# Four x buffers instead of three, earlier load slots, and a new table of turns in a fused Fourier layer and MLP

## The chip, the cores and the metric

The kernel runs on one core of a Trainium2 chip. The core has five engines that work from their own instruction queues, each in order: TensorE (PE in the profile, with its weight loads as PEld), VectorE (DVE), ScalarE (ACT), GpSimd (POOL) and SyncE (SP). SP and POOL issue the DMA transfers of this kernel, which run on 16 DMA engines. TensorE writes into PSUM banks of 512 fp32 columns, and ACT or DVE must empty a bank before TensorE can use it again. The metric is the device time of one execution in microseconds; lower is better. A table of runs gives the median of several executions; the profile is one further execution.

## What is computed

Two stages run one after the other. The first works on 8 sequences of 3008 positions and 256 channels: a Fourier transform along the sequence, one complex 256 x 256 product, a soft threshold, and the inverse transform. The second treats the 24,064 resulting rows as tokens of an MLP with 2048 hidden units whose activation is a squared relu.

```python
X = np.fft.rfft(x, axis=1)                   # x: (8, 3008, 256)
Yr = Xr @ w_r - Xi @ w_i + b_r
Yi = Xr @ w_i + Xi @ w_r + b_i
Yr = np.sign(Yr) * np.maximum(np.abs(Yr) - 0.01, 0.0)   # Yi likewise
y = np.fft.irfft(Yr + 1j * Yi, n=3008, axis=1)
h = y.reshape(24064, 256) @ w_in             # w_in: (256, 2048)
r = np.maximum(h, 0.0)
out = (s * (r * r) + b) @ w_out              # w_out: (2048, 256)
```

## The kernel before

**The transform of one batch.** 3008 is 94 x 32, so the transform is a product of small Fourier matrices in four steps.

1. `s1_units(b)`: 16 units. Each multiplies a piece of x (94 partitions x 512 columns) by `A_t` into a PSUM bank and evicts it to a tile `u`. A tile of four positions is written to a DRAM buffer `ud` (L784).
2. `take_rows` reads `ud` back, turned, as four tiles `us` (L802), and `s23_units(b)` works on them: `fwd_unit` (matrix `F_t`, result `xf`), `sum_unit` and `mix_unit` (the complex product, with three real products in place of four, into `ring`), `shrink` (the soft threshold: three DVE instructions, L899, L903 and L907, then moves of quarters by SP, L918, or for the last pairs by DVE copies, L924), and `inv_unit` (matrix `T_t`, result `v`, written to the DRAM buffer `vd`, L955).
3. `take_half` reads `vd` back as two tiles `vs` in four transfers (L972).
4. `s4_units(b)`: 14 units with the matrix `C_t` write the rows `yt` that the MLP reads.

**The MLP.** Tokens are cut into tiles of 512. A tile has 16 slots, and in slot `mc` `first_mm` computes 128 hidden units of it: two matmuls of 512 columns into `psh`. After each second slot the two banks of `psh` get one relu (L1154 on ACT or L1156 on DVE, result `rt`) and one square (L1163 on ACT or L1165 on DVE, result `gt`). The second product of tile i runs in the slots of tile i+1. Most tiles use a scheme of seven block products in place of eight (`seven_mms`). It needs sums of quarters of `gt`, four for each half of a tile (`s_op`, L1325 on DVE); the fourth may also be an accumulating DMA from `gt` to `gt` issued by POOL (L1317). Results leave PSUM through L1390 or L1278 on DVE into `ost` and are stored by SP (L1189).

**The order around it.** The first batch is transformed alone (`first_batch`, about the first 46 us). From then on the units of the next batches' transforms are put into the slots of the MLP of earlier batches: `plan` and `aside` are dictionaries from a slot number to work, `mark[b]` is the first slot of batch b's own tiles, and in the loop over b the names `s0`, `s1`, `s2` are `mark[b-2]`, `mark[b-1]`, `mark[b]`. So step 1 of batch b runs from `s0 + 36` to some 14 slots ahead of `s1` (8 for b = 2), its rows are taken around `s1`, steps 2 and 3 run from `s1 + 2`, and step 4 in the last 15 slots ahead of `s2`. This fixes TensorE's order. Every instruction of another engine (an eviction, relu, square, sum, transfer) is a "piece": `later` appends it to `pieces`, and `TURNS` has one entry for each of the 2693 pieces, two base-36 digits whose value divided by four is a delay in pieces, and whose remainder is the engine (ACT, DVE, SP, POOL). `plan_turns` sorts the pieces by number plus delay, and `pump` emits them in that order between the matmuls.

**Buffers of x.** x of a batch is read from DRAM as four tiles, chunks of 8 positions, by POOL, with a conversion to fp16. From batch 2 on `load_x_later` issues each tile as two transfers, halves, of 188 KB in fp16 (L350). The tiles rotate through `xpool`, which has three buffers; the fourth chunk of batches 0 and 1 has a buffer of its own (`x2pool`), later used by `T_s`. With three buffers, the fourth chunk of a batch takes the place of its own first chunk, and its load waits for step 1 to have read that one. Only the first chunk of batch 2 has a gate: a one-element copy (L348) that waits for the `us` rows of batch 1.

Of the kernel before, what the change touches and what calls it, by code (L numbers as in the profile page):

```python
# [27 lines left out]
    "101c0x111515141h1l14181k3o181l1x5m5m750x151h1l2e2q1u1i0g0t0g0s7x0p0t11192y1q2226080w2g0h110l"
    "111h1p3e2m2u220h0t0g1c0x1h212d2i2q3a3q0h101g0g250h3q4q0l191l1x2m3m321q0c0w1g0c0p0x1d292x3q32"
    "3y36101w091e0c0p1h0o390x1h1p252m323q3a0k0s1831523i0l0x111l1t212e2u3m36080m0c0w0k1829182o1519"  # L30
    "1h1t362u3m260o0s1p101s111h1l1x263a2i2q15321k2g154e3q0o151d25292t45453l0c0k1k0l0t1h21292h292l"
    "2t081e0d0i0g3h0h0s212h143i1g1m1k1n371g1s2g1h3e4m101a2i2q3m3q0w120s0x1s113q101p0x111g1l1m181h"
    "1g1k201l3i4y1h1m252t1c3x1h191c451c1c20191e1x11143p1x191k2814151c1q192q141o2g1d1l1k2h1h4u1c1p"
    "1p1o1x2d2p1g1x4236181824152e1865141l11161e1x2h143415182p1b1c301t151i181p291d141p1h1k291p1o24"
    "1l1n6j1k2d1l1l1k1o1h2p1x261h1t1c1w1f5v1h1p1x2d2m2u2y3i101g0x160w1h2h0x2l0w181d0x1n1o2o1t110s"
    "1t1z1x1l1x292d2u2i3e2y0g1w1110182d182p1d1g1w1d1f5b1p1o202p1l1x1g1x1h2y1g1o1h292t454i564i5a18"
    "1u0o180l0u0h1l29101g0l143h0r111g2s1d0p0s1f1p0w142l111h184a191l21252d2u2m3u2u0w200w3q0w1h100t"
    "101t1c201p2p113t141i1p26191g1w1d1t1w281x261f4b1d1h252l1h25393h4q423i4214240l0k6y0r0s3u0s2k0t"
    "0l0o0z0l0t0w1l1011141o2k191h1p293p4l294l292t1x2p0g0u0k200l0w1i0l102d0x1t0x19264i1e102y1g2h0w"
    "1g1y1k28192q1i15292t181k2k1h151e3e3m1f2k2u142s1h0x1l1d141p18191g1t2m2a1o1y1o2g1d1p1s291p1p24"  # L40
    "1p2y1o1t1s1y1o211p1q252h1k1o2w1t1k1z1k1s3g1t1l1o1z1x1h1s291p1p1q1o1x241k1t242o1p3e1l1p1o1p2h"
    "1p2t1c1l2y1h1g2h1d1i1g1w1h1m252l1o2g1l2t391j1g311t1d1620291n1d141o1h1w1w1x20241p3f7b1l1t1l1x"
    "1o1s1d1p2h461h1p1c1s1b5v191l1t213q262e2u0w1g0t0y0w1h2h0x2t0w181d0x1n1s1w1p0x0w1t1n1p1p1t2l2p"
    "3a3m2m3q0w1g150w191g14291t181s191b5j1x1h1k1w1x211h1p252a1k1o1h252l495m4i4q4y0x1q0w180t0y111l"
    "2d101g0x0w190z15142g1h0x141j1h101l3c142h1k46191h1p252l3u2u3u2u0o0w111a0w28190x181918202d3l11"
    "191d3a253a191g1k1d1l1o201l1q174b19251x2d1d2t3d3l3u4m3y460o1g0x0o4i0z0k3u182w0p0h0k0v110p0o18"
    "0w1519181w191h292h3h2x4d4d4l49292h0l3a0o1w0d0o120l0o210p3x0k111a1y1e0t6m0s2c0w102a1c1x1d3a2a"
    "1a1m0x1x2p181c2s1l1c1m363u1j282m0s2k190p2t150w1l190x14282m4i191i1428111l1l211t2l1c1t2q1g2l1h"
    "1q1c1s191i2h2t1d1k3d1p1g1v1g202s1x1h181z1p1g1o2k1l1x1q1s1t211o1w202s1x1m1t1x1o1w2p1l1x1l1t2y"
    "1t1k281l1q1o211l1q252l1o381l2c351j1g2x1x191a1c1x1r1h18251l1s1w1w24281p1r7b1x251h1p1o2o1p1x1l"  # L50
    "3u1g1t1g2k1f5v1d1h1l1t22262y2i0s1d0t2y0o1p2h0w2t0w281d0p1j0w2k1p0x101t1n1p1p2d2h3l3u424a4m08"
    "1s0t0x0w1h101p1p141k11137719181c1w191d1c1l1p3m1o2k1d1l1p293q463a260w160w1g0x260t1t2h182g0p0t"
    "290z1514251x11181z251k1s2o1g211s3m1d1p1t252d3e3m42260w18112e1g2s100t1c151g1t113d193p1c1q1x36"
    "191c1p1h1k1k241l1u1b4r181l212d1l2l353p4e4u4i3q0s380t0s160z0k160s1c150t0s171d11101t101d1k1o24"
    "1l1p1x2t41413d3d2t4h393h0w160w1c0l0t0y0p142l11450l11524m3q1m1y0u005y042410101e101p151u1i120t"
    "1t2h1014281h181i3a3e2p2d2m0o2h190l3l150w140x11141k2m3u1t1y1c28191d1g211d3d1w1h2q1g1l1k1q1g1t"
    "1h22292t1c1g3c1x1g231g1k341x1d1k231p1g1k2k1l1p1q1p1t2h1o1t1s2s1p1q1s1x1o1s251p2h1l253y1k1k28"
    "1h2a1k1x1h1i212h1k3c1h242l1f1c2w1x15161g211r1p18241p1t2g1s1t2c1x1n7f1g1x1x1h1s2o1p1p1x4e1g1t"
    "1c2k1f5z1d1h1l1t2u1y2e3e0s1d0t1i0o1p2h0w2x0w341d0p1j0w1o1t0x101d1r1p1p1x2d2d2q362m3e0c1w0t10"
    "102g181d211g211d1f5b211o1o3h1p291k1t1h1q1c1s1l1p2t454i5e4q4y151a0s1g0t160s1p29101g0p103t0r11"  # L60
    "1g2o1d0p0s1f1h0w1g2c0w19192a1d1h252l2x4m3m322q111c103e18240x111415141s1t2h0x3h151q1t2e15141s"
    "1g1p202g1p1y1f4j1h1p252p1l292x3t4i4q423m142c0l0k0y0r0w3y0w240x0p0s0z190x0w280x191c1c2o1d1l1p"
    "25412x2d4d2p3t3t250o2u0o210l0x3u0l0o350p210k1d2q0s0y0o2p0w141m182c1d221g292p1c1o2w1l1o1y3a3a"
    "452d2m1429190p2h150w1s0x1114281u3y1t221828191h1o1x1l21201p2y1c241l1u1g1x1d1u2h2t1k1s3o1p1d1v"
    "1g1o2k1x1h1k1z1x1l1c2l1p1t1m1t1w241l1s212k1p421o1t1k1o2g2h351d1h1q1c1d211c261g1s1d1i212d1o34"
    "1p202l351c301p155y181t1j19101p1h1k211p1o241x1n771g251l1l1k1s1h1p214q1h1t1c1s1b5v1d1h21253q32"
    "2i260s140p0u0l212h0w1l0s180p0t2t1c2g1p0x1c1l1n1p1h252l393u3e3y46081g0x0w191g141t19182d19135b"
    "1d141c1w191t1c1x212y1g291h1p2h3x4q564a3q0s1u0s180p0u0s1h1x101k0x142x0v0x1g2k1h110s311d141828"
    "191l1l6e1l1p1x2h2t3a4e3m2q0w19103i101k180t0s11181s1d2h0x3x141e1h2y0x181o151l1s201h1q174b1925"
    "252h192x3d3p3y4u4e3y0o340d0w4a0n0o0y0o180t0l0o0z1d0t0s1p10191g1k1w1h1x2d2p49354h414h412p2d0d"  # L70
    "120o180l0s2a0p101o0x410h1p565a1u080u0h2c0o0s1q181x19222a362u121a0p1p2d0w102w1d141e363e252c2m"
    "0k28110h2x110o281w11151h2q2y1x261g28151l1c251h2d1l1x2y1k1o212a1k1x1h26252t181g301t1k1z1k1k2w"
    "1x1h1k2x1p1g1p2k1k1l1m1p1o2g1l1t1s2s1p3u1l1p1p1o2g1l1p1g253a1h1h211c2e1g1s1d1i21291o2g192l2p"
    "1j1k2o1l1d5m20291f151c201h1p251o1o201l1o2p1x1l1k1s1l3h1l3e1h1p1c1o1h1l1t2132363e2a0w1k0t0y0w"
    "1p21182p1c2k1t15231c3g211h181t391p1t1x252h323q322e0s0w1110151g10291t1g25151l201k1x2l311o1x1p"
    "3a1c1o1h2h454h525i5a4e111q0o180p0y0k1h1p141k0p141d0v19183119111f1h0w141c1o1x1519252935424a3i"
    "320o1o103y101g11151d1c1k0x1h112h1p2y19102c181c1x191y1c25252h1l2t393h4q4a3i3q0s2k111b0o4m0o10"
    "110p140z111d0w201d141c2c191h1p2h353d3l392h293l290g1o0l0p0u0l0o2c0t2h1d461i1u220o28151x261g1t"
    "1d2i221q212l20142g1518223a3e2d1c2h1l0t1n1d1g1w1h1g1p363a1k1s1l1p1s211h1l1l1u1k1t1w211t222h2t"
    "1k1o3c1p1h1v1g1o3d251h1k231h1g1k291l1p1p1o2g1o1s212o1l1k211p1o2o1p2l1k1p1u1l1p291k4d411k1w1h"  # L80
    "1m1x291k24191j1g2h1p191x1l1c1w1d1g251o281p1x1o1x21251x261g241o211p1y252h1o2c1l1r1o2o1x1h391t"
    "1k1o1p1p1t1s1w1p1t1w2d1l1t1x221k211s1w1x2225291s2t1d1r1s2g1t1l1v1l1o211t1w241s2g1p1t1s281p1p"
    "212a1l1x1o1w1x2225251s2c1d2h1o2g1p1h1v1l1s241t1t1x1w201t1x20291p1t1t2e2y1u1u321c1l1o1s1l1q21"
    "291o2g191n1s2o1t1l2t1p1o1o1p1p1t1s2c1p1t1s251p1t212u1o1t1s1w1p1u25291o2t1d1r1s2s1t1l1v1l1o1s"
    "1t1t241s2h1p1t1t1s1t1y1w281s251p1q1x1y21261p1u1x1y"
# [1501 lines left out]
```

## Time and profile before

| | us |
|---|---|
| median of 3 runs | 814.78 |
| lowest and highest | 814.72, 814.84 |
| profiled execution | 814.47 |
| its span, first to last instruction | 812.4 |
| mean granted TensorE clock in it | 0.997 of full |

The profile shows, for each engine, how long it was busy; for a group of instructions, the line, engine, operation, tiles (out<-in), count, then busy time and mean duration in ns, then the idle time before them and what ended it. A row of a timeline has the start, the duration and the instruction, with a count when several were merged; a bracket tells how long the engine sat idle before it and what released it. A row of the waits names who waited for whom, with the total, the number of times and the longest. SPq rows are the sequencer of SP issuing transfers.

The span has five main loads: 1792 of TensorE's matmuls write `psh` (444.5 us busy, with the later ones overlapping), 4,032 of them `psa` from `gt` (344.1 us in two groups); ACT has 347 relus (355.0 us) and 259 squares (272.2 us); DVE has 117 squares (141.2 us) and 279 sums (190.8 us in three groups). The 65 accumulating transfers take 4.0 us from issue to landing in the median, from 3.2 to 8.7. The halves of x issued on L350 take 5.5 us in the median, from 3.9 to 8.1.

### The profile page before, as it was taken

The page shows a single profiled execution, that of the slowest core. Times are in us where ns is not written, and L with a number is a line of the kernel's source. Part 1 is how long each engine was busy: PE and PEld are TensorE (multiplying, and loading weights), DVE is VectorE, ACT ScalarE, POOL GpSimd, SP SyncE. Part 2 cuts the span into 40 slices and gives each one's busy share as a digit, 9 for nine tenths or more (in the row PEclk, how much of TensorE's full clock was granted, in tenths as well). Part 3 has the DMA queues.
Part 4 walks back from the last instruction along what each step waited for, and adds up shares of the span by engine and source line. Part 5 has one row for each costly group of instructions (what it writes and reads, how often), then busy time and mean ns, then how long its engine had stood idle before and what let it go on. Part 6 is the DMA issues. An engine that isn't in the chain of part 4 may idle for free.

```text
span 812.4 us, 22159 instructions
## 1 busy us (share of the span) xinstructions
PE 801.9 (99%) x9006; PEld 614.0 (76%) x9006; DVE 760.4 (94%) x1334; ACT 748.9 (92%) x938; POOL 108.7 (13%) x153
## 2 busy tenths in 40 slices
...
GB/s 201 182 173 89 92 243 150 115 138 166 222 122 120 151 154 232 100 123 179 121 209 113 158 153 145 169 125 143 140 162 117 141 98 115 176 70 54 78 55 90
DMA packets 121054, 113.42 MB, mean 140 GB/s; under 512 B 9965, under 2 KB 98161, under 8 KB 120953
## 3 DMA queue, kind: packets, MB, share of 16 engines
...
## 4 chain that ended last, share of the span: by engine, by line
PE 55%; DVE 3%; DMA 1%; issue 0%; DVEq 0%
PE psh L225 24%; PE psa L225 20%; PE psf L225 11%; DMA gt<-gt 1%; DVE gt L1325 1%; DVE ost L1390 1%; DVE ring L924 1%; DVE gt L1165 0%; DMA out_dram<-ost 0%; DVE v L288 0%; DVE u L288 0%; DVE s L1325 0%; DVE rt L1156 0%; DVE ost L1278 0%; DVE ring L907 0%
## 5 line engine op out<-in xcount | busy, mean ns | idle before, releaser
L225 PE MATMUL psh<-yt,w_in 128*128 128x512 f16 (+3 forms) x1792 | 444.5, 343 | 0.2 <-ACT rt L1154 0.2
L225 PEld LDWEIGHTS <-gt 128*128 128x128 f16 x4400 | 306.5, 98 | 143.8 <-DVE gt L1325 3.9
L1154 ACT ACTIVATE rt<-psh 128x1024 f32<-128x1024 f32 x347 | 355.0, 1025 | 25.6 <-PE psh L225 22.9
L1163 ACT ACTIVATE gt<-rt 128x1024 f16<-128x1024 f32 x259 | 272.2, 1061 | 3.4 <-DVE rt L1156 1.4
L225 PE MATMUL psa<-w_out_t,gt 128*128 128x128 f16 (+1 forms) x2208 | 199.9, 224 | 0.3 <-DVE gt L1165 0.3
L225 PEld LDWEIGHTS <-w_in 128*128 128x128 f16 x1824 | 151.9, 98 | 15.9 <-issue 1.5
L225 PE MATMUL psa<-T_s,gt 128*128 128x128 f16 x1824 | 144.2, 219 | 0.3
L1165 DVE TENSOR_TENSOR gt<-rt 128x1024 f16<-128x1024 f32 x117 | 141.2, 1217 | 2.5 <-ACT rt L1154 2.1
L1317 POOL DMA_DIRECT2D gt<-gt x65 | 56.5, 868 | 574.2 <-DVE s L1325 157.7
L1390 DVE SCALAR_TENSOR_TENSOR ost<-psa,s_bc,bias_bc 128x256 f32<-128x256 f32 x152 | 72.8, 479 | 7.8 <-PE psa L225 6.7
L1325 DVE TENSOR_TENSOR gt<-gt 128x1024 f16<-128x1024 f16 x107 | 73.0, 683 | 0.6
L1390 DVE SCALAR_TENSOR_TENSOR ost<-psa,s_bc,ost 128x256 f32<-128x256 f32 x129 | 61.7, 478 | 4.8 <-PE psa L225 4.0
L880 DVE TENSOR_TENSOR ring<-psf,s 128x512 f16<-128x512 f32 x84 | 57.6, 686 | 4.0 <-PE psf L225 2.5
L1325 DVE TENSOR_TENSOR gt<-gt,s 128x1024 f16<-128x1024 f16 x86 | 59.0, 686 | 1.2 <-PE psf L225 0.4
L1325 DVE TENSOR_TENSOR s<-gt 128x1024 f16<-128x1024 f16 x86 | 58.8, 683 | 0.4 <-ACT gt L1163 0.2
L225 PEld LDWEIGHTS <-s 128*128 128x128 f16 x688 | 45.4, 98 | 17.6
L225 PE MATMUL psa<-T_s,s 128*128 128x128 f16 x688 | 52.4, 219 | 0.0
L225 PE MATMUL psf<-W_g,xf 128*128 128x256 f16 x336 | 50.4, 273 | 0.0
L225 PEld LDWEIGHTS <-xf 128*128 128x128 f16 x504 | 44.8, 98 | 3.3
L350 POOL DMA_DIRECT2D x<-in_x_dram x48 | 32.3, 766 | 78.6 <-PE psa L225 39.6
L225 PE MATMUL psf<-x,A_t 94*96 94x512 f16 x103 | 39.3, 381 | 0.3 <-DVE u L288 0.2
L225 PE MATMUL psf<-C_t,vs 96*128 96x96 f16 x484 | 38.3, 205 | 0.9 <-DMA vs<-vd 0.6
...
## 6 DMA issues: line engine op xcount, KB each, us to landing
...
ring<-ring SPq DMA_DIRECT2D x120, 64.0 KB
```

Source lines behind the costliest of these rows:

```text
L225: return nc.tensor.matmul(out, lhs, rhs, **how)
L350: nc.gpsimd.dma_start(out=t[0:N1, i * w : (i + 1) * w], in_=xv[:, at : at + w])
L880: lambda e: nc.vector.tensor_tensor(out=ring[0][:, i % 4], in0=ps, in1=hold[i // 2][:, i % 2].unsqueeze(1).to_broadcast([P, 2, D]), op=ALU ...
L924: lambda e, o=o[:, k], a=a[:, k]: nc.vector.tensor_copy(out=o, in_=a),
L1154: nc.scalar.activation(out=rt, in_=ps, func=AF.Relu)
L1163: nc.scalar.activation(out=gt, in_=rr, func=AF.Square)
L1165: nc.vector.tensor_tensor(out=gt, in0=rr, in1=rr, op=ALU.mult)
L1317: nc.gpsimd.dma_start(out=a12, in_=a11, accum_op=ALU.add)
L1325: nc.vector.tensor_tensor(out=out, in0=a, in1=b, op=op)
L1390: ins = nc.vector.scalar_tensor_tensor(out=out(), in0=hold[of], scalar=s_bc[0:size], in1=other(), op0=ALU.mult, op1=ALU.add,)
```

## The change

Three things change. `xpool` gets four buffers. The loads of x and of `us` rows get other slots: for batch 2 the fourth chunk is asked for at slot 24 and not 55; for batches 3 to 7 the four chunks at -8, -6, 10 and 26 slots from the mark of the batch two before, and not at 10, 14, 26 and a computed slot; the four row loads at -9, -6, -4 and -1, and not at -9, -6, -1 and 4. The table `TURNS` is new throughout: 2693 entries as before, the mean delay is 16.0 pieces and was 17.0, and 869 pieces go to ACT (875 before), 1269 to DVE (1261), 444 to SP (444) and 111 to POOL (113).

```diff
 TURNS = (
-    "1x1x261s291p1t221o291s1w291l1u2m2q2y321c1t1c1c25191c291d1s1c282w1o1t1k20353n6z3r6f173r111521"
...
+    "1t1t221o251l1p1y1k251o1s251h1q2i2q362q181p18181t151820181p1c203o1l201g1l294f7b1b3b1b3j15151h"
...
 )
@@
-    xpool = ctx.enter_context(tc.tile_pool(name="xp", bufs=3))
+    xpool = ctx.enter_context(tc.tile_pool(name="xp", bufs=4))
@@
-            assert b < 2 or (b, c) in held[-3:]
+            assert b < 2 or (b, c) in held[-4:]
@@
-    for c, at in enumerate((18, 18, 18, 55)):
+    for c, at in enumerate((18, 18, 18, 24)):
         aside.setdefault(at, []).append(
             lambda c=c: load_x_later(2, c, [] if c else [row_loads[(1, 3)]])
         )
@@
-        for q, at in enumerate((-9, -6, -1, 4)):
+        for q, at in enumerate((-9, -6, -4, -1)):
             aside.setdefault(s1 + at, []).append(lambda t=take_rows, q=q: t([q]))
@@
         if b + 1 < B:
-            free_at = 37 + 4 * (mark[b] - s1 - 50) // 16
-            for c, at in enumerate((10, 14, 26, free_at)):
+            for c, at in enumerate((-8, -6, 10, 26)):
                 aside.setdefault(s1 + at, []).append(
                     lambda b=b, c=c: load_x_later(b + 1, c)
                 )
```

The table's entries decide both where a piece stands in its engine's queue and which engine takes it, so nearly every queue is in a new order, while the matmuls stay in theirs.

More of the change, by code (lines that the diff above doesn't have):

```diff
@@ L26 @@
 TURNS = (
-    "1x1x261s291p1t221o291s1w291l1u2m2q2y321c1t1c1c25191c291d1s1c282w1o1t1k20353n6z3r6f173r111521"
[L28 to L85, printed above, removed]
+    "1t1t221o251l1p1y1k251o1s251h1q2i2q362q181p18181t151820181p1c203o1l201g1l294f7b1b3b1b3j15151h"
+    "101p1x0w11150w201h0w14182w192h3h5m564v7j590l0p0x111m12221i000h042c7h0d0l0p0t1u121a1y040o1o08"
@@ new lines @@
+    "0p0d0t19213e262e2q050p0w2c0l1519212a2y3a2e080s280c0l2t3y4a090p0t1h2a2y2i1m081029090l0t1h2529"
+    "3m4e2q2e0w1g002i040o191c3811191h1x3i2u1y420o0w181p4y260h0t0x1d1h1x262u361y04360s180p0x2p141s"
+    "11151d1h3e2q2a2u0g111l0w1g111h1t292e3e2e2q0t360s182p363e0l0x19191h413p2x31080w1t0c0p151t2d2d"
+    "352t35081e080q0c350k0w1k2k101y111a1c1k1l2k2d2i32141e2i2u3i4i0w160t0s1p153i101o0x1x141g1i151g"
+    "1l1k1s1h3m4y191i1t2p111s1t10181v15203s141m1x0x102l1p191p2t14181c1m1d2q101c341f63191l1c1s1h3e"
@@ new lines @@
+    "175n1d1d1h181l212l3u0x1h1q2y0s0s1w0p260s450s1d0t0y161l210w2w0x1w2h0z0w2k1h0t0w1h3t1d0w1w1d1l"
+    "1s1l1p201t1j5z1c1l1l1l1k1o1h1x1l321g1p1g2c1h1h1p212i36222i0s1s0p0u0s2d2l1g310p340x1517141s1x"
+    "19101h1v1t1x252935423m4a320g1p0x0w101c101p15141k150z5r1l15181w1d21181l192y1k2k1h1h1p2d3e2i3q"
+    "2q0s3q0o110p0y0k1l2d0w1k0t0w3t0z151s2d1p0x0w1v1l1c1s201g1x1l3q191l1t1x2h3m3a4m2e0s180w161828"
+    "0x11141518201529151p196q1t1y19181s1c1h1s241h1q1h21212h19212l3d463y4m3a10240d0c4a0n0o0y0o2d11"
@@ new lines @@
+    "0l0o13150p0s1k0w0x101k2k191h1p2149354d3125312d250c2y0g100h0p0y0p102g1t3d0h1p4i2a1u0c0u0g2k0w"
+    "1d2i1g25151e1m11212h0w1g2c1d1g1q3a3u3l2d2m0s2g190l1d11101l101114282e3y191i1420111h1l1x1l2p1g"
+    "1p1y1c1g1h1u1k24191u2d2h1d1o3k1d1h1j1k1o2k1t1h1g1r1h1p1g2k1h1l1m1p1x2h1j5v1c1l1k201h3y1f5z1c"
+    "1p1d1c1o1t251615192q1d141w151a181l15161t29182w191c291b182w1l1114211j1h101t1d1o291p1o241l1n6z"
+    "1k1t1l1t1k1t1l2h1t1y1c1l181o1h1x25293m2q2y260w1g0t0y0w1x29102h14240p0x39102g1p0x101h1n1p1h1p"
@@ new lines @@
+    "29313q363q3y0c1k0x0w1019181x15141g150z6z1l19181o1p1x151l213a1g1k1d1l1x1x2a363e3m0w3q0w180l1y"
+    "0s1l2d14380h0l150r11142s1l0x141r1h141h2s1c251d421h1h1p2d2h3y3i2u2e0o0x0w3m101s0x0l0w1h0w1k21"
+    "2d0l3t0x2m1l260t0w1k141h1s241d1q1h1l2h2x1h1x293h463m464e10240h0g460r0s120s30190x0o17190t0w1l"
+    "101114182k191h1p212x4d2h2x3p1t1t2d0g6e0k1s0h0s2i0h0s2g1l3p0l111u164e0o420s290p191i141w111a1i"
+    "1m1u0p1p290k142o1d141i3a3a3h2d2i0k2c150d1d110k1t1d0x0w202q3u1x26142011191c25191l1w1h2y1c1s1g"
@@ new lines @@
+    "1q1p24151q2d2p181d381l1c1r1c1w2x1t19181v1l1c1l2g1g1p1i1o1o2h2j6f1d1h1g2o1d1e1f631g1l1c1g2k1d"
+    "1p2215191i1h14211d1i1k1s191i1t1x1g3015292917182x19111o21130t0w1p191o2c1o21281h1j771c2d1h1l1o"
+    "2k1d1h1t1y181l182c1h1l252d2m3m2m2u0w1k0t0y0p1p2h0t2l0w281d0p1n0w2k1t0x0w1p1r1p1p1x2l35424a3i"
+    "320c1l0t1010180x311h101c110v5b191g0w1h112d181p1x22101g19293p414e4m5e4u0w1m0w180l0u0l191l142w"
+    "0l0k0x0r0x0w30190p0w1f1p0s0w290x1d1g6q151d1t2d3h4u3y423e0w150w4u0w1c0s0t0w11141c0t1x0t290p2u"
@@ new lines @@
+    "113u0h0g100k11181k151q111x1x2l0x212x3d4i423e3q0g20050s460f0s3q0s2w0x0l0k0z150t0s1h0w0x10141s"
+    "191h1x254l2x3l292p3d3p2p0h1q0o100l0o0y0p142c39410l0x221m4m0y1y4m081y08250h112i101w0x1a1i1m0s"
+    "1t2d0s1c281d1c1m3q3u3125560s20150d1b11141h1l1118202a3y101a101w111d1h1o1h1t1h1p2q181l1c1m1c1o"
+    "1h222d2p1d1g351l1d1r1c1k2w1t1d1g1z1l1c1g2s1k1p1i1p1o1w1n6b1h1l1x2k1h3i1f4z1c1h181c2819292m11"
+    "151e140x201016181p191m1p251c301d2d2x1f101c1d0t1s2131150w1s191p281k1k241h1j771d1p1t1l1o2g1l1t"
@@ new lines @@
+    "1h321c1l1c2g1d1h1p2d2u323i2a0s190p0u0s1p2h0w2h0w1w1d0p1j0w381t0x1g1p1r1t1l1x2d353q3y4a320c0s"
+    "0t10111d143d1h101c110v571910182g1519181l192q14281d1h4d4l4u5i525i0t120o110l1210191t142s0l0k0x"
+    "0r0t0s2o150t0s170x0o0w2h0x1h142i0t191d252p3q463q4q0o1k0w4q0s1g150t111h141c2d2l0t290x1215260l"
+    "0o140t1g1k1w1h221h1x252l1925313h3q4a3y4e142c0l0k1m0r0s120s34110p0w171h11101p1419181g201h1p1x"
+    "252x3l3t2x311x3h1t0p4q0o100l0o3q0p0w2c1t3h0l0p320k0y0k250w191i181w0x1a11212p101k2w1l1k1y3a3u"
@@ new lines @@
+    "1j2c2m102g190l1d150w211g1115282e2i1c1m1824151h1l291p2p1k1l2u1g1k1l1u1k20191m292d1d1o301d1h4t"
+    "1g1k291p1d1c1r1h181o2d1l1p1i1k1l1s2b5z181l1c1s1h46175f1d1p19181t1h212q101h1q0w101s101i141h11"
+    "1i1p25182s1d1s2t1f102p1d0t1l1x2d150s1w191g1w1p24281p1j6z1h2l1h1t1k2g191p1d42181l182l1d1h1l1t"
+    "263a2i220s180t160o252l102h102w150t1f0w2s1p15141l1n1t1h1p292h3a3q2i36081o11111024111d1p102s15"
+    "17571d1w1c1x191d1g1p1x261k2l191l1x4l4q52565a0o1m0s1g0p0u0s1h1t141w0p0o3t0v0t0s1o190t0x1f110s"
@@ new lines @@
+    "181s0x2118720t111x2d2p2u4a3a2q0h1c0s4q0s1w0p0t0w0x0w1k2d310p2l0x1i0x1i0x0w1c0x1d1c1w1d1i1g1t"
+    "212l191h3d3p3y424a4i1020110g0q170s3y0w1c150p0p171d0t18200s151d1024191h1p214l294125292x2l2l0c"
+    "220w1w0h0s1a0h0s28313p0p1h4y1i4y0t5y0o2g0p111a0w1p1122321e1i1y0q0c1h250c102k19101e323e35292i"
+    "0g250x09190t0c1s100t10281y2i1t221824151h1l211p2p1k1t2i1g1k1l1u1k21191y292h1c1k381h1g1n1k1o3d"
+    "1t1h1g1v1l1c1l211g1l1m1o1o2c1l1o1s2g1h3a1h1p1h1k2g2h2t2215191e1c1128142a1g1x1d1i212d1k301h20"
@@ new lines @@
+    "2l1f1c2o1p151c251n1d141x1h1s201o1p241p1o211l1p1s251p391l1u1g1t1k1s1l1p1x2d3m2u322a101k0x1210"
+    "1h29142l18241d111n14381t1h1o1x1x1h1t292h313i323y3m0k0w0x0x0w1c111l151424111t141c2t111p1d1x1p"
+    "1u1c1s1l252d455m4q5246105y0w1g0t0y0w1d1h101s0p142d0r110s20110p13150p0s290w1p15151h2d314e3y36"
+    "3e0g0w191i0s100p141h181o0x25141h1136191c1o1h1p1w1p1y1c1l212h1h212t354a3u363e0o100t13143m101k"
+    "110t0w13151d141g191h1k1w1h1l1t213x2x253d3l251t1t0s1s0p0s2y0p0o1w152t193y1a3e1e0k240l191m1820"
@@ new lines @@
+    "151i1m1q212h1k0x2s151s1y3236290w281h0t1j190w1s1d1h2036361c1t1d1h1k241h1p1d1m181l1s241p1u2d2h"
+    "1d1o381d1h1j1k1o2d1p1h1k1v1h1g1o2c1p1p1p1o1x1l1s1s291p1p1p1o1s1w1x2d1h1p2q1p1g211h39411c1o19"
+    "1e1t211g20151f1c2g1l19291l1c1g1h1h211o2d1l1t1k1s1l1x1x2u1g1t1k1o1p1u1x251k28151n1o2d1t1h2p1l"
+    "1k1w1h1k1p1o2l1l1p1o1w1l1l1p1u1s1s1t1w1p1y21251o28191n1o291t1h2p1l1k1x1l1k1o1o2c1l1p1o241l1l"
+    "41421h1l1k1o1h1m1t1x1g2d151f1g1o1h192p1d1g1w1d1c1p1o1w1l1t1w291l1p1p2u2e1u1m1u141h1k1s1l1y21"
@@ L86 @@
+    "211o2k19391k1s1l1d2d1h1h1t1h1g1k1o281l1p1o1x1l1x3l3q1g1l1k1o1h1m1t1x1g24151f1g2d1h192d1d1g1w"
+    "1h1k2c1o1s1l1p1p1t1x1y1k241o211l1m1t1u1x221l1q1t1u"
 )
```

## The prediction

> **What bounds the kernel now.** I read the first part of the page, then the waits of TensorE, then the timeline of TensorE where a wait falls, then the queues beside it.
>
> ```profile
> PE 801.9 (99%) x9006; PEld 614.0 (76%) x9006; DVE 760.4 (94%) x1334; ACT 748.9 (92%) x938; POOL 108.7 (13%) x153
> ...
> L1163 ACT ACTIVATE gt<-rt 128x1024 f16<-128x1024 f32 x259 | 272.2, 1061 | 3.4 <-DVE rt L1156 1.4
> ...
> L1165 DVE TENSOR_TENSOR gt<-rt 128x1024 f16<-128x1024 f32 x117 | 141.2, 1217 | 2.5 <-ACT rt L1154 2.1
> ```
>
> TensorE is busy 99%, but its ends are modelled, so short stalls hide in "busy". I took the start of every matmul, subtracted the start of the one before, and subtracted that shape's usual step: 56 ns for 128 columns, 109 for 256, 216 to 220 for 512, 42 for 96 (medians of this trace). What is left above 25 ns is stall. It adds to 10.9 us: 5.6 in the first 46 us (before the table of turns applies) and 5.3 after. The granted clock is 0.997 of full, so no time lies there. 814.47 us (the profiled run) therefore cannot fall much below 809.2 by any reordering. Of the 5.3 us, 0.55 lie before 55 us, 0.03 at 108.7, and the rest at places like these:
>
> ```profile
> 398.11 0.50 PE L225 MATMUL psa<-w_out_t,gt 128*128 128x128 f16 x6
> 398.82 0.38 PE L225 MATMUL psf<-ring,T_t 128*128 128x256 f16 x2 [0.20 <-DVE u L288]
> ...
> 402.81 0.59 PE L225 MATMUL psh<-yt,w_in 128*128 128x512 f16 x2
> 403.48 0.62 PE L225 MATMUL psa<-T_s,gt 128*128 128x128 f16 x8
> ```
>
> Six matmuls of 56 ns starting at 398.11 end their steps at 398.45; the next starts at 398.82: 0.37 us lost (the row admits 0.20). Two of 216 ns from 402.81 end at 403.24; the next starts at 403.48: 0.23 lost, to the sum on L1325. Such a run stands where one batch's transform hands over to the next. By the same subtraction the six runs cost 0.64 us (200 to 205), 0.39 (299 to 304), 0.65 (398 to 403), 0.68 (497 to 503), 0.73 (596 to 602) and 0.58 (693 to 698): 3.67 together. VectorE has no gap there:
>
> ```profile
> 396.17 1.23 DVE L1165 TENSOR_TENSOR gt<-rt 128x1024 f16<-128x1024 f32 x1
> ...
> 398.09 0.68 DVE L288 CAST u<-psf 96x512 f16<-96x512 f32 x1
> 398.69 1.21 DVE L1165 TENSOR_TENSOR gt<-rt 128x1024 f16<-128x1024 f32 x1
> 399.82 0.68 DVE L1325 TENSOR_TENSOR gt<-gt 128x1024 f16<-128x1024 f16 x1
> ```
>
> Starts, not durations, say what a row costs its queue: the square holds VectorE 399.82-398.69 = 1.13 us, an eviction 398.69-398.09 = 0.60. Two more stalls are transfers, 0.77 us at 115.13 and 0.24 at 327.86:
>
> ```profile
> PEld L225 <- DVE gt L1325: 3.9, 9, 0.6
> ...
> PEld L225 <- DMA vs<-vd: 0.8, 1, 0.8
> ```
>
> ```profile
> 101.93 1.02 POOL L350 DMA_DIRECT2D x<-in_x_dram  x2 [39.56 <-PE psa L225]
> ```
>
> ```profile
> 103.43 2.05 SPq L955 DMA_DIRECT2D vd<-v  x2
> 106.51 1.96 SPq L784 DMA_DIRECT2D ud<-u  x2
> 111.34 0.78 SPq L972 DMA_DIRECT2D vs<-vd  x2
> ```
>
> SP's last write of vd goes out at 105.12 and the read of it only at 111.34, 6.2 us later. The fourth tile of x for batch 2, held on POOL until its buffer was read, goes out at 101.93 and 102.44 and lands at 107.58 and 109.18, just in that stretch. For the last batch, with no x in flight, the same wait is 2.46 us (697.16 to 699.62).
>
> **The change, part by part.** In the two built programs TensorE's 9,006 matmuls and weight loads stand in the same order, so all of them cost nothing; only who serves them moves.
>
> *Engines.* Net over the program, 18 squares go from DVE to ACT, 8 relus from ACT to DVE, 10 evictions of 512 columns and about 8 of yt from ACT to DVE, and 2 sums from POOL's transfers to DVE. ACT: 18 x 1.061 - 8 x 1.025 - 10 x 0.585 - 3.7 = +1.3 us. DVE: -18 x 1.217 + 8 x 1.220 + 10 x 0.683 + 4.4 + 2 x 0.683 = +0.5 us. In total nothing; place matters.
>
> *The six runs.* I counted VectorE's queue, in both programs, from the last shrink of a batch (L899, as at 389.54) to the L1325 sum that TensorE waits for. Runs 1 and 3: one square fewer, one v more: -1.13+0.60 = -0.53 us. Run 2: one square and one u fewer, two v more: -0.53. Run 4: two squares fewer, three u more: -0.46. Run 5: one relu fewer, two v more: +0.07. Run 6: one square and one v fewer, one relu more: -0.60. A run can give back no more than its stall: 0.53+0.39+0.53+0.46+0+0.58 = 2.49 us. Bounds: 0 (each sum waits for something else) and 3.67. I take 2.49, as these VectorE rows follow each other without idle time. The square that went to ACT there is covered: ACT's rows between 386.6 and 406 take 18.7 us of 19.4 before and 18.3 after.
>
> *x loads.* The load at 55 becomes one at 24, ahead of the vd writes, and the wait on POOL goes. Up to 0.77 us is won at 115.13, since the read of vd needs to go out only 0.8 us earlier. Against it SP's queue now has a store of 0.65 us (L1189) ahead of the read. Bounds 0.77 and 0; I take the middle, 0.39. From batch 2 on, the first halves of two x tiles go out 6 to 8 slots ahead of a batch's mark, not 10 to 14 behind it. On POOL they stand behind the two L1317 sums there (316.77 and 319.08), so neither sum is issued later. With four buffers no x load waits for TensorE: the batch before has read its tiles 8 to 14 slots ahead of the mark, the first of them earlier. SP sends two row loads beside these sums in place of three in the run at 317, where the 0.24 was lost (issued 319.08, landed 327.82, 8.74 us against a median of 4.0). Bounds +0.24 and -2.1 (the rival below); I take +0.12.
>
> *Half rows (us).* They are asked for at -9, -6, -4, -1. The first is due 13 us after its issue at 317 (330.2), beyond the longest landing here, 8.7: nothing. Their L1325 and L288 consumers don't move.
>
> *The start.* Three halves of x(2) now stand earlier on POOL, one ahead of the gate on low, two among the sums of w_out (L521). The first must wait for a landing at 30.85, so W_g is 1.4 us later, but the sums of w_out still begin with the landing of w_out at 38.52. Two issues of 0.64 put their end from 47.89 to 49.2; TensorE asks for it at 53.49. Cover gone, it would cost the overrun alone. Nothing.
>
> *New tight places.* At 152.6 VectorE has a relu where an eviction stood: its queue from the relu's release at 147.87 to the L1325 sum takes 1.13+0.60+0.60+0.60+0.40+0.60+0.20+0.68 = 4.81, ending 152.68 where 152.54 is needed: 0.15 lost. At 751.58 a relu on ACT stands behind a square released 0.18 later than the one before: about 0.16. Bounds 0 and 1 us; I take 0.31.
>
> Sum: 2.49+0.39+0.12-0.31 = 2.69 us off 814.47, that is 811.78. The median of the runs is 0.31 above the profiled execution: 812.1.
>
> **Rivals.**
> 1. *The stalls only move.* A sum that comes 0.5 us earlier waits for ACT's square instead, and the gain is nil. For it: ACT is at 92% and gets the squares. Against it: ACT's rows in run 3 end earlier too. Time: 814.47-0+0.31 = 814.8. Chance 0.20.
> 2. *x and the sums share the DMA engines.* Four or more L1317 sums land beside the moved halves. At 61 to 68 us x halves landed 0.9 to 1.6 us apart; two of them would put the sums 2.1 us later if the engines divide themselves. Room was -0.04 us at 327.86, 2.09 at 427.06 and 2.12 at 228.57, so only one sum is hit: +2.1, 814.2. Against it: the sums are first in their own queue. Chance 0.10. The Trainium skill, "DMA: Bandwidth & Descriptors", section "Queues, rings and completion order", says each engine takes turns between queue rows packet by packet. By that rule the x halves take from SP's row loads and stores, not from sums ahead of them in the same row, and this trace's 8.74 us beside three row loads agrees that the queues share; it would leave the sum of 812.1 as it is and speaks against this rival.
> 3. *Slower: relus caught behind squares on ACT.* Two squares stand next to each other on ACT 24 times before and 38 times after, 14 more. A relu released behind the first waits up to 1.06 us, and TensorE has just two psh banks. From the end of an ACT relu to the matmul that takes its bank the median room is 0.98 us, a tenth of them have under 0.48. It decides once the relus behind a pair have less room than 0.98: at 0.48 it costs 14 x (1.06-0.48) = 8.1 us, which gives 812.1+8.1 = 820.2. For it: TensorE waits for ACT relus at 50.00 (0.40 us). Against it: a table can put a pair where a relu has room. Chance 0.13.
>
> **How the numbers follow.** Forecast 812.1, chance 0.57, own range 809.5 (all 5.27 us gone) to 813.1. A difference under 0.2%, 1.6 us, counts as none: below 813.15 is faster, above 816.4 slower. Faster 0.57; same 0.30 (rivals 1 and 2); slower 0.13 (rival 3). The range 809.5 to 816.0 leaves out rival 3 alone.
>
> **What would show it.** Right: run 3 has no bracketed wait of psf<-ring,T_t on VectorE near 398 and the six runs lose 1.2 us or less together; vs<-vd is gone from the waits of PEld; POOL's x rows (L350) wait for no PE. Rival 1: the same total with ACT as releaser of gt. Rival 2: gt<-gt among the releasers of PEld, landings above 9 us near 217, 317, 416. Rival 3: psh<-yt,w_in waiting for ACT rt all along. A TensorE order or granted clock other than before's would make the whole sum wrong.

## The result and the profile after

| | before | after |
|---|---|---|
| median of the runs, us | 814.81 (6 runs, 814.24 to 816.35) | 810.08 (6 runs, 809.96 to 810.97) |
| profiled execution, us | 814.47 | 810.04 |
| its span, us | 812.4 | 808.2 |
| stall of TensorE after the first 46 us, us | 5.3 | 1.17 |

The ratio of after to before is 0.9947, with a 95% interval of 0.9936 to 0.9957: 4.7 us less. Of the two profiled executions the later one is 4.43 shorter, 4.1 of it in the span (812.36 to 808.24, unrounded).

The first part of the page of the kernel after, its busiest groups, and the chain of work that ended last:

```profile
span 808.2 us, 22126 instructions
...
PE 799.2 (99%) x9006; PEld 613.1 (76%) x9006; DVE 758.9 (94%) x1342; ACT 749.4 (93%) x932; POOL 107.0 (13%) x151
...
PE 93%; DMA 0%; ACT 0%; DVE 0%; issue 0%; DVEq 0%; ACTq 0%
...
L1163 ACT ACTIVATE gt<-rt 128x1024 f16<-128x1024 f32 x277 | 289.6, 1059 | 3.1 <-DVE rt L1156 0.7
...
L1165 DVE TENSOR_TENSOR gt<-rt 128x1024 f16<-128x1024 f32 x99 | 120.0, 1216 | 2.4 <-ACT rt L1154 2.1
```

Eighteen squares went from VectorE (117 to 99) to ScalarE (259 to 277), yet the busy time of both moved by less than 2 us. The share of work did not change; the places did. In the chain TensorE holds 93%: hardly any other engine's row stands in it. The 55% that the same line gives for the kernel before can't be set beside this, since that chain is followed back only to 319.08, and this one to 45.01.

The waits of TensorE after the first 46 us: first those of its weight loads, in total, number of times and longest, in us:

```profile
PEld L225 <- DVE gt L1325: 2.4, 7, 0.5
PEld L225 <- issue: 0.7, 2, 0.5
```

and those of its matmuls:

```profile
PE psh L225 <- ACT rt L1154: 0.2, 1, 0.2
```

The wait for `vs<-vd` (0.8) is gone from the weight loads, as are that for `gt<-gt` (0.3) and the one for the square on L1165 (0.7). A weight load that waits is not yet a stall: the waits above add to 3.1 us, and less was lost. By the subtraction of the prediction (start to start, less the shape's usual step) 1.17 us are left in eight places: 0.11 at 47.47, 0.40 at 50.03, 0.10 at 54.87, 0.06 at 302.26, 0.04 at 410.23, 0.17 at 499.58, 0.20 at 694.10 and 0.10 at 744.38.

The third run, where the prediction showed two stalls, on TensorE after the change:

```profile
396.14 0.50 PE L225 MATMUL psa<-w_out_t,gt 128*128 128x128 f16 x6
396.47 0.38 PE L225 MATMUL psf<-ring,T_t 128*128 128x256 f16 x2
...
400.42 0.60 PE L225 MATMUL psh<-yt,w_in 128*128 128x512 f16 x2
400.86 0.61 PE L225 MATMUL psa<-T_s,gt 128*128 128x128 f16 x8
```

Six matmuls of 56 ns begin at 396.14, and the next begins 0.33 later: no gap, where 0.37 were lost. Two of 216 ns from 400.42 take 0.44: no gap, where 0.23 were lost. The same matmul that began at 398.11 begins at 396.14, and the one that began at 403.48 at 400.86. Since the two traces are level at 50 us (a matmul that began at 50.00 begins at 50.03), these 1.97 and 2.62 us are what had been won on the way.

VectorE and ScalarE in the same stretch:

```profile
395.98 1.21 DVE L1165 TENSOR_TENSOR gt<-rt 128x1024 f16<-128x1024 f32 x1
397.12 0.68 DVE L1325 TENSOR_TENSOR gt<-gt 128x1024 f16<-128x1024 f16 x1
397.72 0.68 DVE L1325 TENSOR_TENSOR s<-gt 128x1024 f16<-128x1024 f16 x1
398.32 0.68 DVE L1325 TENSOR_TENSOR gt<-gt,s 128x1024 f16<-128x1024 f16 x1
```

```profile
395.34 0.57 ACT L288 CAST u<-psf 96x512 f16<-96x512 f32 x1
395.90 0.58 ACT L288 CAST v<-psf 128x512 f16<-128x512 f32 x1
396.39 1.06 ACT L1163 ACTIVATE gt<-rt 128x1024 f16<-128x1024 f32 x1
```

The eviction of `u` for which TensorE waited on VectorE is on ScalarE, two rows ahead of a square. VectorE's rows still follow each other without idle time; what differs is which rows it has and their order.

Last, the loads of x. The waits ahead of POOL's L350 rows in the kernel before and in the kernel after (total us, times):

```profile
  PE psa L225: 39.6, 1
  PE psf L225: 38.1, 5
```

```profile
  DMA x<-in_x_dram: 1.1, 1
  issue: 0.3, 1
  POOL x L348: 0.3, 1
```

and SP's queue near the write and read of `vd` in the kernel after:

```profile
105.19 0.36 SPq L955 DMA_DIRECT2D vd<-v  x1
...
107.69 0.61 SPq L1189 DMA_DIRECT2D out_dram<-ost  x1
109.49 0.33 SPq L972 DMA_DIRECT2D vs<-vd  x1
```

No x load waits for TensorE any more. From the last write of `vd` to its read 4.3 us pass (6.2 before); of that, by the profile's waits of SP, the read itself waits 1.0 us for the writes to land, and waited 2.8 before. The store of L1189 that now stands ahead of the read is issued by 108.30, over a microsecond before the read can go.

### The profile page after: what moved, and what is told of

Read it like the earlier page. It is cut to its first block, busy times and chain, and to the rows that moved or that the text cites. A ratio compares the mean times of both kernels' runs of the same rounds, so it can differ in the third digit from the quotient of the medians.

```text
span 808.2 us, 22126 instructions
## 1 busy us (share of the span) xinstructions
PE 799.2 (99%) x9006; PEld 613.1 (76%) x9006; DVE 758.9 (94%) x1342; ACT 749.4 (93%) x932; POOL 107.0 (13%) x151
## 4 chain that ended last, share of the span: by engine, by line
PE 93%; DMA 0%; ACT 0%; DVE 0%; issue 0%; DVEq 0%; ACTq 0%
PE psh L225 40%; PE psa L225 34%; PE psf L225 19%; DMA out_dram<-ost 0%; DVE ost L1278 0%; ACT rt L1154 0%; ACT u L288 0%; DVEq L1278 0%; ACTq L1154 0%
## 5 line engine op out<-in xcount | busy, mean ns | idle before, releaser
L1154 ACT ACTIVATE rt<-psh 128x1024 f32<-128x1024 f32 x339 | 346.9, 1025 | 23.7 <-PE psh L225 21.5
L1163 ACT ACTIVATE gt<-rt 128x1024 f16<-128x1024 f32 x277 | 289.6, 1059 | 3.1 <-DVE rt L1156 0.7
L1317 POOL DMA_DIRECT2D gt<-gt x63 | 54.8, 870 | 650.0 <-DVE s L1325 194.3
L1165 DVE TENSOR_TENSOR gt<-rt 128x1024 f16<-128x1024 f32 x99 | 120.0, 1216 | 2.4 <-ACT rt L1154 2.1
L1325 DVE TENSOR_TENSOR gt<-gt 128x1024 f16<-128x1024 f16 x109 | 74.4, 682 | 0.7
L1325 DVE TENSOR_TENSOR gt<-gt,s 128x1024 f16<-128x1024 f16 x86 | 58.8, 684 | 1.4 <-PE psf L225 0.8
L1325 DVE TENSOR_TENSOR s<-gt 128x1024 f16<-128x1024 f16 x86 | 58.7, 683 | 0.5 <-ACT gt L1163 0.2
L1156 DVE TENSOR_SCALAR rt<-psh 128x1024 f32<-128x1024 f32 x37 | 45.0, 1219 | 3.3 <-PE psh L225 1.6
```

Of the source, the lines that this page charges most:

```text
L1154: nc.scalar.activation(out=rt, in_=ps, func=AF.Relu)
L1156: nc.vector.tensor_scalar(out=rt, in0=ps, scalar1=0.0, scalar2=None, op0=ALU.max)
L1163: nc.scalar.activation(out=gt, in_=rr, func=AF.Square)
L1165: nc.vector.tensor_tensor(out=gt, in0=rr, in1=rr, op=ALU.mult)
L1317: nc.gpsimd.dma_start(out=a12, in_=a11, accum_op=ALU.add)
L1325: nc.vector.tensor_tensor(out=out, in0=a, in1=b, op=op)
```

## The experiments

Each was run beside the kernel before on the same chip; "before" is its median there: 814.43 (27 runs) for experiments 1 to 4, 814.6 (16 runs) for 5 to 8 and 814.6 (17 runs) for 9 and 10. Stalls are by the subtraction of the prediction. In the table of turns an entry's value divided by four is the delay, its remainder the engine: 0 ScalarE, 1 VectorE.

**1. Buffers and slots alone.** The code of the kernel after with the order and the engines of before for everything but the loads of x and of `us` (so the table is re-written too; not shown):

```diff
-    xpool = ctx.enter_context(tc.tile_pool(name="xp", bufs=3))
+    xpool = ctx.enter_context(tc.tile_pool(name="xp", bufs=4))
...
-    for c, at in enumerate((18, 18, 18, 55)):
+    for c, at in enumerate((18, 18, 18, 24)):
...
-        for q, at in enumerate((-9, -6, -1, 4)):
+        for q, at in enumerate((-9, -6, -4, -1)):
...
-            for c, at in enumerate((10, 14, 26, free_at)):
+            for c, at in enumerate((-8, -6, 10, 26)):
```

> Four x buffers and the new slots, with the old table's order and engines for every other piece. Theory (the six VectorE runs give 3.2 us, the transfers 1.0): only the transfers' part comes, about 1.0 us off 814.8, so 813.8; the stalls at 115.1 and 327.9 are gone, the six runs still lose 3.5 us or so. Rival A (the earlier loads take waits off the queues, and the table only follows them): nearly the whole gain, 810.1 to 811. Rival B (the moved halves of x delay the accumulating transfers): 814 to 817, with gt<-gt among TensorE's releasers.

Measured: 814.92 (813.73 to 818.09, 10 runs) against 814.43, ratio 1.0006, interval 0.9996 to 1.0017. The six runs still lose 3.7 us and the wait for `gt<-gt` near 327 is gone, but the stall for `vs<-vd` grew to 1.91 us in the profiled execution (the slowest of the ten; its start was 2.5 us longer, so its times lie that much later). Its POOL queue:

```profile
104.44 0.51 POOL L350 DMA_DIRECT2D x<-in_x_dram  x1 [40.15 <-PE psa L225]
110.81 0.51 POOL L350 DMA_DIRECT2D x<-in_x_dram  x1 [5.85 <-PE psf L225]
```

These are first halves of batch 3, asked for 6 to 8 slots ahead of the mark. They went out as soon as their buffers had been read, in the stretch that the change had just cleared of the halves of batch 2. The read of `vd` went out at 112.84 and TensorE got its first half at 119.02, 6.18 us later; before, 3.79 (111.34 to 115.13). The 1.0 us that the theory expected did not come: alone the slots win nothing. An x half had been issued 2.0 us ahead of this read. The Trainium skill, "DMA: Bandwidth & Descriptors", section "Queues, rings and completion order", says that a DMA engine takes turns between the queue rows it has work for, a packet at a time. Whether that is the reason for the 2.4 us more is not shown: in the eighth experiment a half goes out 2.1 us ahead of the same read, and the read is in time.

**2. The table alone.** The kernel before, three buffers and old slots, with the new order and engines for everything but those loads (new entries throughout):

```diff
 TURNS = (
-    "1x1x261s291p1t221o291s1w291l1u2m2q2y321c1t1c1c25191c291d1s1c282w1o1t1k20353n6z3r6f173r111521"
...
+    "01010i000l01010a000p000c0x01061a1e1i1i000l00000l01000k0009000k2s01100001192f672j5v032v01010l"
...
```

> Three x buffers and the old slots, with the new table's order and engines for every piece but the loads of x and us. Theory: the runs' part comes, about 3.2 us off 814.8, so 811.6, with the stalls at 115.1 (0.77) and 327.9 (0.24) still there. Rival A: less than 1 us off, 813.8 or more.

Measured: 812.26 (811.42 to 812.96, 6 runs), ratio 0.9968, interval 0.9955 to 0.998. The six runs lose 0.42 us, the same as in the kernel after (0.43). But the wait for `vs<-vd` near 115 grew from 0.77 to 1.49:

```profile
116.50 0.39 PE L225 MATMUL psf<-C_t,vs 96*128 96x96 f16 x5 [1.33 <-DMA vs<-vd]
```

Another 0.29 is lost at such a read at 412.59. These 1.78 us, against 0.04 in the kernel after, are most of the 2.2 between the two medians.

**3. Only the fourth load of batch 2 earlier.** The kernel before with four buffers and that one load moved; the table re-written so that all else keeps its turn:

```diff
-    for c, at in enumerate((18, 18, 18, 55)):
+    for c, at in enumerate((18, 18, 18, 24)):
```

> Before, with four x buffers and the fourth load of batch 2 asked for at slot 24 and not 55; nothing else moves. Theory (that load delays the last writes of vd): the stall of 0.77 us at 115.1 goes, and the read of vd is issued about 3 us sooner after its last write; 814.0. Rival (the order of SP's own queue sets it): the stall stays at 0.5 us or more and the time at 814.8.

Measured: 813.6 (813.11 to 814.2, 10 runs), ratio 0.999, interval 0.998 to 0.9999. The stall near 115 is gone; the runs (3.7) and the wait for `gt<-gt` (0.38 at 327.57) stay. SP's queue:

```profile
103.15 2.71 SPq L955 DMA_DIRECT2D vd<-v  x2
...
109.48 0.77 SPq L972 DMA_DIRECT2D vs<-vd  x2
```

The read goes out at 109.48, 1.86 us earlier than before and 4.0 us after the last write of `vd` at 105.50 (6.2 before; about 3 us less were expected, 2.2 came). 0.83 us come off the median, as much as the stall of 0.77, though the interval reaches from 0.1 to 1.6.

**4. Six squares to ScalarE, nothing else.** The kernel before with one row per run changed from VectorE to ScalarE in its place (the square that the new table gave to ScalarE there; in the fifth run a relu); one of the six entries, 1w from 1x:

```diff
-    "0w1519181w191h292h3h2x4d4d4l49292h0l3a0o1w0d0o120l0o210p3x0k111a1y1e0t6m0s2c0w102a1c1x1d3a2a"
+    "0w1519181w191h292h3h2x4d4d4l49292h0l3a0o1w0d0o120l0o210p3x0k111a1y1e0t6m0s2c0w102a1c1w1d3a2a"
```

> Before, with six entries of the table changed by one: in each of the six runs one square (in the fifth one relu) goes from DVE to ACT at the same place in the order. Theory (what stands in VectorE's queue ahead of the sums decides): each run loses 1.1 us of queue, so most of its stall goes, 3.7 us together; 811.5. Rival (the wait moves to ACT, whose relus are caught behind the squares): the six runs lose as much as before or more, with ACT as releaser, 814.8 to 817.

Measured: 815.42 (814.55 to 817.77, 10 runs), ratio 1.0014, interval 1.0005 to 1.0024. The runs lose about 3.9 us, as much as before, and in the first one the stall has changed its name:

```profile
201.82 0.59 PE L225 MATMUL psh<-yt,w_in 128*128 128x512 f16 x2 [0.34 <-ACT rt L1154]
```

```profile
198.35 1.08 ACT L1163 ACTIVATE gt<-rt 128x1024 f16<-128x1024 f32 x1
199.29 0.61 ACT L288 CAST v<-psf 128x512 f16<-128x512 f32 x1
199.76 1.10 ACT L1163 ACTIVATE gt<-rt 128x1024 f16<-128x1024 f32 x1
200.72 1.97 ACT L1154 ACTIVATE rt<-psh 128x1024 f32<-128x1024 f32 x2
```

The square at 199.76 holds ScalarE for 0.96 us (200.72-199.76), and the relu behind it frees the `psh` bank 0.51 late. VectorE's sums did come earlier: the weight loads waited 3.9 us for L1325 before, and here

```profile
PEld L225 <- DVE gt L1325: 1.2, 5, 0.3
```

What was won there went to waits for relus and evictions on ScalarE. The waits of 0.36 at 199.34 and 0.37 at 398.16 stayed, since the `u` that ends them stands on VectorE ahead of the square that was moved. A square less on VectorE, by itself, buys nothing.

**5. The new engines in the old order.** The kernel before with the new table's engine for all 51 pieces of the six runs that changed theirs, each in its old place; one of the changed rows:

```diff
-    "0l0o0z0l0t0w1l1011141o2k191h1p293p4l294l292t1x2p0g0u0k200l0w1i0l102d0x1t0x19264i1e102y1g2h0w"
+    "0l0o0z0l0t0w1k1011141o2k191h1p293p4l294l292t1x2p0g0u0k200l0x1i0l102c0x1t0x19264i1e102y1g2g0w"
```

> Before, with the new table's choice of engine for the 51 pieces of the six runs on which the two tables differ (squares to ACT, evictions to DVE and some back), each at its old place in the order. Theory (what counts is that the square goes to ACT together with evictions that come to DVE, and the order is secondary): the six runs lose 1.2 us or less in place of 3.7; 812.0. Rival (the new order is needed as well): they lose 2.5 us or more; 813.5 to 815.5.

Measured: 816.96 (816.03 to 817.53, 10 runs) against 814.6, ratio 1.0026, interval 1.0016 to 1.0035. The runs lose 6.1 us, more than either theory allowed, and wait for rows of many kinds:

```profile
PE psa L225 <- DVE ost L1390: 1.0, 2, 0.7
PE psh L225 <- ACT rt L1154: 0.9, 2, 0.7
PE psf L225 <- DVE ring L924: 0.6, 1, 0.6
PE psf L225 <- DVE u L288: 0.5, 2, 0.3
```

**6. The six rows back to VectorE in the kernel after.** The reverse of the fourth; one of the six entries, 1x from 1w:

```diff
-    "101114182k191h1p212x4d2h2x3p1t1t2d0g6e0k1s0h0s2i0h0s2g1l3p0l111u164e0o420s290p191i141w111a1i"
+    "101114182k191h1p212x4d2h2x3p1t1t2d0g6e0k1s0h0s2i0h0s2g1l3p0l111u164e0o420s290p191i141x111a1i"
```

> The changed kernel, with six entries turned back: in each of the six runs one square (in the fifth one relu) goes from ACT to DVE. Theory (VectorE's queue ahead of the sums is tight again): about 0.5 us returns in each run, 3 us together; 813.1. Rival (the new order leaves VectorE more than 1.1 us of room): below 1 us returns; 810.1 to 811.0.

Measured: 818.19 (818.07 to 818.61, 4 runs), ratio 1.0043, interval 1.0028 to 1.0058. Six entries out of 2693 cost 7.9 us against the kernel after with its late load (810.27), run beside it. The runs lose 6.8 us, 1.1 each, about what a square holds VectorE (1.13); in the first:

```profile
202.04 0.45 PE L225 MATMUL psa<-w_out_t,gt 128*128 128x128 f16 x5 [0.67 <-DVE gt L1165]
```

A transfer of `gt` comes late too, 1.10 at 709.28. The direction was right and the size double: VectorE has no room in these runs in the new order either.

**7. The fourth load of batch 2 at the old slot, with four buffers.** The kernel after, all else in its turn:

```diff
-    for c, at in enumerate((18, 18, 18, 24)):
+    for c, at in enumerate((18, 18, 18, 55)):
```

> The changed kernel, with the fourth load of batch 2 asked for at slot 55 as before, still with four buffers. Theory (a load goes out when its queue is free and its buffer read, whatever its slot): with a buffer free since 46 us it still goes out near 63 us, nothing is lost; 810.1. Rival (the slot sets when it goes out): it goes out near 102 us, the stall near 115 comes back with about 1.5 us; 811.6.

Measured: 810.27 (809.97 to 811.01, 4 runs), ratio 0.9946, interval 0.9931 to 0.9961: the kernel after, but for 0.2 us. POOL's queue:

```profile
59.10 2.06 POOL L350 DMA_DIRECT2D x<-in_x_dram  x4 [0.29 <-POOL x L348]
```

The load asked for at slot 55 went out with the others near 60 us, 40 us ahead of where the kernel before had it. POOL runs ahead of TensorE; a load waits for its buffer and for what stands ahead of it on POOL, not for its slot. Between the two slots POOL has nothing else to issue, so in both traces every engine's rows stand in the same order. Of the change at this place the fourth buffer counts, and the new slot does not. The profile also shows how much two executions of the same rows can differ: 0.39 us is lost here at 411.11 for `vs<-vd`, and 0.04 at that matmul in the kernel after.

**8. The first sum on POOL given to VectorE.** In the kernel after the first halves of batch 3 stand behind a sum on POOL that needs VectorE, and so go out at 118.94. Entry 291, the remainder from 3 to 1:

```diff
-    "1l1k1s1h3m4y191i1t2p111s1t10181v15203s141m1x0x102l1p191p2t14181c1m1d2q101c341f63191l1c1s1h3e"
+    "1l1k1s1h3m4y191i1t2p111s1t10181t15203s141m1x0x102l1p191p2t14181c1m1d2q101c341f63191l1c1s1h3e"
```

> The changed kernel, with one entry changed: the first sum that POOL issues (near 118 us) goes to DVE. On POOL the first halves of two tiles of batch 3 stood behind it. Theory (that sum's wait is what keeps these loads out of the last transfers of vd): they go out near 104 and 110 us as in the slots-alone kernel, and TensorE waits 1.0 to 1.9 us for vs near 115; 811 to 812. Rival (the loads do not matter there, or the slot holds them): no such wait; 810.1 to 810.5.

POOL's queue in the kernel after, and then in this one:

```profile
118.35 0.94 POOL L1317 DMA_DIRECT2D gt<-gt  x1 [57.41 <-DVE gt L1325]
118.94 1.42 POOL L350 DMA_DIRECT2D x<-in_x_dram  x2
```

```profile
102.34 0.51 POOL L350 DMA_DIRECT2D x<-in_x_dram  x1 [41.10 <-PE psa L225]
108.44 0.51 POOL L350 DMA_DIRECT2D x<-in_x_dram  x1 [5.58 <-PE psf L225]
```

Measured: 811.27 (810.86 to 813.43, 7 runs), ratio 0.9964, interval 0.9952 to 0.9975. The loads moved as expected, and the read of `vd` went out 1.1 us later than in the kernel after (110.57 for 109.49), but TensorE did not wait for it near 115; by the trace's landings the read took 3.77 us, as in the kernel before (3.75). The time fell into the theory's range, but not for the theory's reason. Against the seventh, run beside it, this kernel loses 1.0 us. Of that, 0.33 at 119.88 is the edit's: a `yt` on VectorE comes late, behind the sum that moved. The other losses can't be put down to it: 0.35 at 411.19 for `vs<-vd` is in the seventh too, and 0.64 more between 50 and 56 us lie long ahead of the row that moved. So the sum does act as a gate for the x loads, but here that gate was worth nothing near 115.

**9. The new order with the old engines.** The kernel after with the old engine for the 51 pieces of the fifth experiment, each in its new place; one changed row:

```diff
-    "0l0o13150p0s1k0w0x101k2k191h1p2149354d3125312d250c2y0g100h0p0y0p102g1t3d0h1p4i2a1u0c0u0g2k0w"
+    "0l0o13150p0s1l0w0x101k2k191h1p2149354d3125312d250c2y0g100h0o0y0p102h1t3d0h1p4i2a1u0c0u0g2l0w"
```

> The kernel after with its own order everywhere, but the 51 pieces of the six runs that changed their engine get the engine that the old table gave them (the new order there without the new choice of engine). Theory: order and engines work only together, as the new engines in the old order cost 2.4 us. The six runs then lose 2 to 6 us in place of the 0.43 of the kernel after, with waits for VectorE and ScalarE both, and the time is 812 to 816 us. Rival: the order alone does it, and the engines are a matter of taste: the six runs lose under 1 us, and the time is below 811.0.

Measured: 815.01 (814.32 to 816.24, 11 runs) against 814.6, ratio 1.0008, interval 0.9999 to 1.0017. The runs lose 5.13 us (0.74, 0.45, 0.71, 1.32, 1.25, 0.66). In the third one the stall of before is back at the same matmul:

```profile
398.24 0.50 PE L225 MATMUL psa<-w_out_t,gt 128*128 128x128 f16 x6
399.01 0.38 PE L225 MATMUL psf<-ring,T_t 128*128 128x256 f16 x2 [0.27 <-DVE u L288]
```

That is the theory's 2 to 6 us. With the fifth this closes the square: old order and old engines 3.67 us of stall in the runs, new engines alone 6.1, new order alone 5.13, both 0.43. The two odd corners differ in the loads of x as well, but by the first two experiments these hardly touch the runs (3.67 and 3.7, 0.42 and 0.43).

**10. Two rows put back.** The kernel after with the `u` at 48.48 put behind the relu at 48.95 on ScalarE, and the `ost` at 497.73 behind the sum at 498.84 on VectorE, against the stalls at 50.03 and 499.58 (entries 10 and 1708; the first is shown, 20 from 1o):

```diff
-    "1t1t221o251l1p1y1k251o1s251h1q2i2q362q181p18181t151820181p1c203o1l201g1l294f7b1b3b1b3j15151h"
+    "1t1t221o251l1p1y1k25201s251h1q2i2q362q181p18181t151820181p1c203o1l201g1l294f7b1b3b1b3j15151h"
```

> The kernel after with two pieces put later in their queue and nothing else: the eviction of u on ScalarE at 48.48 goes behind the relu at 48.95 (0.40 us of stall at 50.03 waits for that relu), and the fp32 output row (ost, L1390) on VectorE at 497.73 goes behind the sum at 498.84 (0.17 of stall at 499.58 waits for that sum). Theory: an engine that TensorE waits for gives back what stands ahead of the awaited row, up to the stall: 0.35 and 0.17, so 809.6 us against 810.1 for the kernel after, both stalls gone from the trace. Rival: the rows put back are late themselves (u frees a psf bank, ost a psa bank), and the two stalls only change their name: 810.0 to 810.6.

Measured: 811.76 (811.27 to 812.92, 7 runs), ratio 0.9966, interval 0.9954 to 0.9977: slower than the kernel after, beyond what the rival allowed. TensorE at the second place:

```profile
497.90 0.59 PE L225 MATMUL psh<-yt,w_in 128*128 128x512 f16 x2
499.67 0.61 PE L225 MATMUL psa<-T_s,gt 128*128 128x128 f16 x8 [1.17 <-DVE ost L1390]
```

The `ost` empties a `psa` bank that the next product needs; started at 499.14 and not at 497.73 it costs 1.33 us where 0.17 were to be won. At the first place 0.40 at 50.03 became 0.24, 0.09 and 0.32 at 49.52, 50.92 and 52.32. None of the ten kernels beats the kernel after.

## Why the prediction was right, and by how much it was off

The forecast was 812.1, and the median is 810.08. The span fell by 4.12 us and the stalls after 46 us by 4.1, which is all of it. The signs named for the forecast came: no bracketed wait of `psf<-ring,T_t` near 398, 0.43 us in the six runs, no `vs<-vd` among the waits, no x load waiting for TensorE.

- *TensorE is the bound, and its hidden stalls are all there is to win.* Right. Its 9,006 matmuls kept their order and the span ends at the same work; the granted clock was 1.0 (0.997 before). The sum by start-to-start steps names the whole change, while "busy 99%" is the same on both pages. The 5.6 us given for the first 46 us do not come out of the steps as stated, which leave 9.5; nothing rests on them, since 9.5 stand there after the change too.
- *Engines: nothing in total.* Right: DVE 760.4 to 758.9, ACT 748.9 to 749.4.
- *The six runs: 2.49 us.* The sign was right and the size too small: 3.24 (3.67 less 0.43). By run, forecast and measured: 0.53 and 0.64, 0.39 and 0.33, 0.53 and 0.65, 0.46 and 0.51, 0 and 0.73, 0.58 and 0.38. The fifth run alone makes the difference: VectorE's queue there grows by 0.07 us by my count, and yet its stall went. The step that failed is the measure itself: I counted how much shorter VectorE's queue becomes up to the sum that TensorE waits for, and took that, up to the run's stall, as the gain. The fourth experiment takes a square (in the fifth run a relu) out of that queue in the same places, the sums come earlier, and nothing is won; the fifth and the ninth show that neither the engines nor the order do it alone. By the matmuls at which it falls, only 1.43 of the 3.67 us stands at the product of the sums (`psa<-T_s`); the other 2.24 are lost at other matmuls, which wait for a `u`, a `v` or a square where the profile names the row. So it is in part luck that the count comes within 0.2 us in five runs: nearly the whole stall went, and the count was capped by the stall. What the experiments fit is that each row has to stand in its queue early enough for the matmul that needs it, on both engines. The tenth shows this for one row (an `ost` behind a sum costs 1.33 us); no experiment takes the six runs apart row by row.
- *x loads at 115.13: 0.39, at 327.86: 0.12.* Both stalls went whole, 0.77 and 0.24; 0.04 came back at 410.23. I had taken the middle because of the store on SP's queue ahead of the read, and this was wrong: the read waits for the `vd` writes to land until 109.49, and the store is out by 108.30. At 115 the buffer was the cause, as the third and seventh experiments show. But the slots win only together with the table: alone they gave 814.92, and the table alone made the wait at 115 worse, 1.49. "No x load waits for TensorE" came true, but not because the buffers had been read: without the sum ahead of them on POOL (eighth experiment) the first halves of batch 3 wait for TensorE, and go out at 102.34 and 108.44.
- *us rows and the start: nothing.* Right within what the traces can tell: a matmul near 50 us begins 0.03 later.
- *New tight places: -0.31.* Neither came. Nothing is lost at 152.6, and nothing at the matmul of 751.58, which begins at 747.48 in the kernel after. The 0.10 at 744.38 is 3.1 us ahead of that one: its relu, at 743.32 on ScalarE, stands behind a square at 742.36.
- *0.31 from the profiled execution to the median.* It was 0.04 this time.

Of the 2.02 us between forecast and median, 0.75 is the six runs, 0.46 the transfers (0.97 for 0.51), 0.21 the tight places, 0.27 the offset; the 0.33 left lies around the span (814.47-812.36 = 2.11 before, 810.04-808.24 = 1.80 after) and in rounding.

The rivals: stalls that only move to ScalarE did not come in this kernel, but are just what the fourth experiment shows where the order does not follow. x halves in the way of the sums did not come either; no wait for `gt<-gt` is left. Relus caught behind squares cost 0.10 at 744.38, and there one square stands ahead and not a pair; the stall before 56 us, 0.60, was 0.55 before the change.

Left open: in the first experiment the halves of batch 3 come with a wait of 1.91 for `vs<-vd`, in the eighth the same halves at nearly the same place (102.34 and 108.44, against 104.44 and 110.81 less the 2.5 us of a longer start) with none. The two differ in the order of SP's stores too, and only one execution of each was profiled; what makes the read take 6.18 us is not known.
